# An expert's row transposes traced in front of the next routing round instead of behind it

## The chip, the cores and the metric

The kernel runs on one core of a Trainium2 chip. The metric is the device time of one execution in microseconds (us). Engines: PE is TensorE (matmuls; PEld its weight loads), DVE is VectorE, ACT is ScalarE, POOL is GpSimd, SP is SyncE, which here only issues DMAs.

## The reference

A linear attention with decay gives 3072 tokens of 384 values each; a mixture of 8 experts then works on them. Tokens go to experts by one global greedy order over all (token, expert) scores, with room for 384 tokens per expert:

```python
for t in range(S):                                   # S = 768, per batch and head
    state = alpha[:, :, t, :, None] * state + np.einsum('bhd,bhe->bhde', k[:, :, t], v[:, :, t])
    y[:, :, t] = np.einsum('bhd,bhde->bhe', q[:, :, t], state)
...
logits = x @ w_gate                                  # x: 3072 x 384, 8 experts
order = np.argsort(-logits.flatten())
for idx in order:
    tok, e = (int(idx) // E, int(idx) % E)
    if assigned[tok] >= 0 or counts[e] >= cap:       # cap = 384
        continue
    assigned[tok] = e
    counts[e] += 1
...
for e in range(E):
    mask = assigned == e
    h = np.maximum(x[mask] @ w1[e], 0.0)             # w1[e]: 384 x 1024
    out[mask] = h @ w2[e]                            # w2[e]: 1024 x 384
```

All data is float32.

## The kernel before, in words

**Attention.** The first 150 us or so compute `x` and its scores `L` chunk by chunk; `x` is written to `x_dram` in HBM. The change does not touch this part.

**Routing rounds.** Instead of sorting, the kernel runs 8 rounds. Each round finds the expert that fills up next, and the score at which it does. `search` (line 565) does it digit by digit, in five steps t = 0 to 4: VectorE compares all scores with a table of digit values (`compare`, line 542, tile `cmp`), TensorE counts with 24 small matmuls (line 591), VectorE tests the counts (`g`, line 592), one more matmul sums the test (line 598), VectorE takes the digit (`k`, line 600) and forms the next key (`nd`, line 603). At the end `es`/`ei` (lines 608, 610) hold the expert's number; SP reads it and issues four DMAs for that expert's weights (`weights`, line 518: two halves of `w1r`, line 525, and of `w2r`, line 527; the pool has two buffers for each). `extract` (line 696) turns the round's token set into a list: VectorE builds one-hot tiles (`hot`, line 712), 24 matmuls (line 722) sum them into a PSUM tile `ix`, VectorE makes `idx` of it (line 724), and GpSimd issues three indirect DMAs (line 729) that gather the 384 rows into `xr`, 128 rows each. `update` (line 633) prepares the next round's scores, with the first comparison, `top` and `cmp`, and the tile `o`. The last round, `search_last`, needs no search.

**Experts.** Expert i is the one found by round i. `prep(i)` (line 765) transposes its rows on TensorE in three groups of three (line 779) into a PSUM tile `xt`; ScalarE rounds each group to `xh` (line 782) and VectorE keeps the rest, `xl` (line 784). A float32 product is made of three rounded ones, so weights are split too: `split` (line 746), per block q of 128 hidden values (8 blocks, q = 0 to 7), ScalarE `whi` (lines 751, 752) and GpSimd `wlo` (line 757); seven buffers of each. The `wlo` splits of an expert wait for given comparisons of round i + 1, by the table `BEHIND`. `ffn1` (line 789) runs 9 matmuls per block (line 795), and ScalarE and VectorE make `hh` and `hl` (lines 799, 800); `ffn2` (line 805), two blocks behind, runs 9 matmuls (line 815). The results go to HBM by indirect DMA (line 826).

**What sets the order.** Each engine runs one queue in order. A scheduler fills these queues from the order in which the code is traced and from priorities; inside `tc.high_priority()` a routing round goes ahead of experts' work. Buffers are handed out in the order of tracing: the pool `psx` has one buffer (`bufs=1`, line 147), which serves the attention's transposes, every round's `ix` (line 717, also named `xt`) and every expert's three `xt` (line 770) in turn. A tile of that pool can be written only when the tile traced before it has been read.

The code traces round 0, round 1, then expert 0's `prep` and blocks; then round i + 1 in front of `prep(i)` for each further expert (lines 833 to 850). Between round 0 and expert 0, `spin_after` (line 553) puts some matmuls without use (line 561) on TensorE.

Of the kernel before, what the change touches and what calls it, by code (L numbers as in the profile page):

```python
# [12 lines left out]
ROUTE_AHEAD = 3  # L13
# [14 lines left out]
def gla_moe_kernel(ctx, tc, q, k, v, alpha, w_gate, w1, w2, out):  # L28
# [10 lines left out]
    E = w_gate.shape[1]  # L39
# [469 lines left out]
    def row(x, w=NU):  # L509
        return x[:, :, None].to_broadcast([128, NU, w])  # L510

    def col(x, n=NU):
        return x[:, None, :].to_broadcast([128, n, x.shape[-1]])
# [35 lines left out]
    st = dict(chu=chu0, o=o0, dig=[dig0[:, t] for t in range(nb)])  # L549
# [83 lines left out]
    def update(i):  # L633
        es, v = st["es"], st["v"]
        nt = st["nt"] + 1
        oh = rw.tile([128, 1], F32, name="oh")
        nc.vector.tensor_scalar(oh[:nt], pcs[:nt], st["k"][:nt], None, op0=OP.is_equal)
        gone = st["rt"][:, 40:48]
        with tc.issue_after(st["tri"].ins):
            nc.tensor.matmul(gone, oh[:nt].to_broadcast([nt, 128]), st["cs"][:nt], start=True, stop=True)  # L640
        nc.vector.tensor_reduce(m_c, L, axis=X, op=OP.max)
        nc.vector.scalar_tensor_tensor(sel_c, v, float(CAP), qe_c, op0=OP.is_le, op1=OP.mult)
        val = rw.tile([128, NU, E], BF, name="val")
        if i + 2 < E:
            sg = rw.tile([128, NU], I32, name="sg")
            nc.vector.tensor_scalar(sg, m_c.bitcast(I32), 31, -2 ** 31, op0=OP.arith_shift_right,
                                    op1=OP.bitwise_or)
            nc.vector.scalar_tensor_tensor(asg, sel_c, es, asg, op0=OP.mult, op1=OP.add)
            nc.vector.tensor_tensor(key_c, m_c.bitcast(I32), sg, op=OP.bitwise_xor)  # L649
            nc.vector.tensor_tensor(val, L, row(m_c, E), op=OP.is_equal)  # L650
            nc.vector.tensor_tensor(di_c, key_c[:, None, :].to_broadcast([128, nb, NU]), shifts,
                                    op=OP.logical_shift_right)
            nc.vector.tensor_tensor(di_c, di_c, masks, op=OP.bitwise_and)
            top = rw.tile([128, NU], BF, name="top")
            nc.vector.tensor_scalar(top, di_c[:, 0], 1.0, None, op0=OP.add)
            for _ in compare(i + 1, top, 0):
                pass
            nc.vector.scalar_tensor_tensor(dig_c, di_c[:, 1:], 1.0, scale[:, 1:], op0=OP.add, op1=OP.mult)
            st["dig"] = [top] + [dig_c[:, t] for t in range(nb - 1)]
        else:  # L660
            nc.vector.scalar_tensor_tensor(asg, sel_c, es, asg, op0=OP.mult, op1=OP.add)
            nc.vector.tensor_tensor(val, L, row(m_c, E), op=OP.is_equal)
        nc.vector.tensor_mul(val, val, col(ramp_c))
        nc.vector.tensor_scalar(un_c, asg, 0.0, None, op0=OP.is_equal)
        ch = rw.tile([128, NU], F32, name="ch")
        nc.vector.tensor_reduce(ch, val, axis=X, op=OP.max)
        nc.vector.tensor_sub(rem, rem, gone)
        chu = rw.tile([128, NU], F32, name="chu")
        nc.vector.tensor_mul(chu, ch, un_c)
        nc.vector.scalar_tensor_tensor(rem, cl_c, 8192.0, rem, op0=OP.mult, op1=OP.add)  # L670
        o = rw.tile([128, NU, E], BF, name="o")
        nc.vector.tensor_tensor(o, col(ramp_c), row(chu, E), op=OP.is_equal)
        st.update(chu=chu, o=o, ch=ch)

    def search_last(i):
        es = rw.tile([128, 1], F32, name="es")
        ei = rw.tile([128, 1], I32, name="ei")
        nc.vector.tensor_copy(es, st["ch"][:, 0:1])
        nc.vector.tensor_scalar(ei, es, -1.0, float(E), op0=OP.mult, op1=OP.add)
        weights(i, ei)  # L680
        nc.vector.tensor_add(asg, asg, st["chu"])
        nc.vector.tensor_scalar(ms_c, asg, es, None, op0=OP.is_equal)
        rts = rw.tile([128, 2], BF, name="rts")
        with nc.allow_low_precision(reason="counts of at most 24 ones"):
            nc.vector.tensor_reduce(rts[:, 0:1], ms_c, axis=X, op=OP.add)
        cum = rw.tile([128, 2, NU], F32, name="cum")
        nc.vector.tensor_tensor_scan(cum[:, 0], ones_c, ms_c, 0.0, op0=OP.mult, op1=OP.add)
        rt = fps.tile([128, 64], F32, name="rt")
        nc.tensor.matmul(rt[:, 16:17], tri, rts[:, 0:1], start=True, stop=True)
        offs = rw.tile([128, 2], F32, name="offs")  # L690
        nc.vector.tensor_copy(offs[:, 0:1], rt[:, 16:17])
        v = rw.tile([128, NU], F32, name="v")
        nc.vector.scalar_tensor_tensor(v, cum[:, 0], offs[:, 0:1], ms_c, op0=OP.add, op1=OP.mult)
        st.update(v=v, v1=None)
# [51 lines left out]
    def split(i, q):  # L746
        hi = fp.tile([128, 2, DB, 128], F32R, name="whi", bufs=7)
        lo = fp.tile([128, 2, DB, 128], F32R, name="wlo", bufs=7)
        a = W1R[i][:, :, q * 128:(q + 1) * 128]
        c = W2R[i][:, q].rearrange("p (a b) -> p a b", b=128)  # L750
        nc.scalar.activation(hi[:, 0], a, AF.Copy)  # L751
        nc.scalar.activation(hi[:, 1], c, AF.Copy)
        with ExitStack() as es:
            if i == 0:
                es.enter_context(tc.issue_after(first_gather[0].ins))
            for h, x in enumerate((a, c)):
                y = nc.gpsimd.tensor_sub(lo[:, h], x, hi[:, h])  # L757
                if i + 1 in compared:
                    after = compared[i + 1][BEHIND[2 * q + h]]
                    tc.add_manual_dep(y.ins, after.ins.name,  # L760
                                      mybir.DependencyInfo(mybir.DependencyClass.Sync, mybir.DependencyReason.DATA),
                                      reason="weights split while the search reads one table at a time")
        CH[i, q] = hi, lo

    def prep(i):
        hi = wp.tile([128, DB, CAP], F32R, name="xh")
        lo = fp.tile([128, DB, CAP], F32R, name="xl")
        for b in range(NB):
            bs = slice(b * 128, (b + 1) * 128)
            o = psx.tile([128, DB, 128], F32, name="xt")  # L770
            with ExitStack() as es:
                if i:
                    es.enter_context(tc.issue_after(F2[i - 1, FB - 3].ins))
                else:
                    st["spin"] = spin_after(WARM_IN_ROUTE[1 + b], *st["spin"])
                    for x in st["spin"]:
                        es.enter_context(tc.issue_after(x.ins))
                for d in range(DB):
                    x = nc.tensor.transpose(o[:, d], XR[i][:, b, d * 128:(d + 1) * 128], ident)  # L779
                if i == 0:  # L780
                    st["spin"] = [x]
            nc.scalar.activation(hi[:, :, bs], o, AF.Copy)  # L782
            with tc.high_priority():
                nc.vector.tensor_sub(lo[:, :, bs], o, hi[:, :, bs])
        XH[i], XL[i] = hi, lo
# [45 lines left out]
        scattered.append(st_)  # L831

    route_priority = [0]
    for n in range(E * FB + 2):
        i, q = divmod(n, FB)
        if i < E:
            if q == 0:
                for r in ((0, 1) if i == 0 else (i + 1,) if i + 1 < E else ()):
                    with tc.high_priority():
                        if r < ROUTE_AHEAD:  # L840
                            tc.cur_priority = route_priority[0]
                        with tc.issue_after(st.pop("hot").ins) if "hot" in st else ExitStack():
                            if r:
                                update(r - 1)
                        search(r) if r < E - 1 else search_last(r)
                        extract(r, 1 if r else 2)
                        route_priority[0] = tc.cur_priority
                prep(i)
            split(i, q)
            ffn1(i, q)  # L850
        if n >= 2:
            i, q = divmod(n - 2, FB)
            if i < E - 1 or q < FB - LAST_BLOCKS:
                ffn2(i, [q])
            elif q == FB - 1:
                ffn2(i, list(range(FB - LAST_BLOCKS, FB)))
            while pending:
                scatter()
# [39 lines left out]
```

## Time and profile before

| | |
|---|---|
| median of 3 runs | 474.49 us (472.36 to 476.5) |
| profiled execution | 476.95 us |
| its span, first to last instruction | 475.2 us |
| mean granted TensorE clock | 0.925 |
| busy: PE, PEld, DVE, ACT, POOL | 411.6, 355.9, 293.3, 193.2, 283.3 us |

In the rows of the profile, a line number names the line of the kernel; `out<-in` are tile names; a time in brackets is how long the engine stood idle before the row, and who ended the wait. Timelines give start and length in us from the start of the span. A table of windows gives, for stretches of time, each engine's busy time, then the granted clock (1.00 is full speed), the share of the DMA engines and GB/s. A list of DMA landings gives the time from issue to landing (minimum, median, maximum) of the DMAs it covers. Matmuls overlap one another, so their lengths exceed their pitch.

### The profile page before, as it was taken

To read this page: it belongs to the slowest core of one execution; us is meant where nothing else is said; L and a number is where in the kernel's file an instruction comes from. 1 tells how busy PE (TensorE), PEld (TensorE's weight loads), DVE (VectorE), ACT (ScalarE), POOL (GpSimd) and SP (SyncE) were. 2 spreads that over 40 slices of the span, in tenths; PEclk is the share of its full clock that TensorE was granted. 3 is DMA by queue.
4 is the path that set the end of the run, shared out by engine and by line. 5 is a ranking of instruction groups with operands and counts; after the bars stand their busy time and mean duration, and the time that the engine had idled before them with its cause. 6 is when DMAs were issued, how large, how long until landed. Compare 5 with 4: busy or idle time off the path is not lost.

```text
span 475.2 us, 10764 instructions
## 1 busy us (share of the span) xinstructions
PE 411.6 (87%) x4142; PEld 355.9 (75%) x4142; DVE 293.3 (62%) x836; ACT 193.2 (41%) x453; POOL 283.3 (60%) x292
## 2 busy tenths in 40 slices
PE   6998899887898643489999999999999969999994
PEld 3776677666677522368987988988988959999993
DVE  7987776767735576766865775875875862222210
ACT  2555554544465322013442352352443434554511
POOL 3886656465510056513894697696796796676802
PEclk8799999899999955569988999999999989999998
DMA  8766656566304653620820631721720825410101
GB/s 258 229 205 200 199 174 208 164 202 188 114 2 173 225 185 134 228 89 1 278 73 17 215 102 51 244 82 44 265 69 34 282 84 153 164 51 0 51 0 52
DMA packets 44595, 65.20 MB, mean 137 GB/s; under 512 B 3328, under 2 KB 26880, under 8 KB 44544
## 3 DMA queue, kind: packets, MB, share of 16 engines
q1 hardware_dynamic: 38304, 50.35, 32.5%
q0 software_dynamic: 3072, 9.44, 6.1%
q10 hardware_dynamic: 3168, 4.72, 2.8%
q8 instruction: 33, 0.54, 0.5%
q14 instruction: 18, 0.15, 0.1%
HBM read 55.06 MB, written 9.44 MB: 136 GB/s over the span
## 4 chain that ended last, share of the span: by engine, by line
PE 57%; DVE 20%; DMA 10%; issue 6%; ACT 3%; POOL 1%; POOLq 0%; DVEq 0%; ACTq 0%; SPq 0%
PE h L795 20%; PE y L815 18%; DMA al<-in_alpha_dram 10%; PE rt L591 6%; DVE sc L234 4%; DVE cmp L542 4%; DVE ga L237 3%; PE xt L360 2%; PE y L323 2%; PE xt L779 2%; PE y L317 2%; PE s L268 1%; PE xt L722 1%; ACT xh L782 1%; DVE vi L699 1%
## 5 line engine op out<-in xcount | busy, mean ns | idle before, releaser
L757 POOL TENSOR_TENSOR wlo<-w1r,whi 128x384 fp32r<-128x384 f32 x64 | 67.9, 1061 | 64.1 <-ACT whi L751 58.5
L757 POOL TENSOR_TENSOR wlo<-w2r,whi 128x384 fp32r<-128x384 f32 x64 | 72.2, 1129 | 4.7 <-DVE cmp L542 3.7
L800 DVE SCALAR_TENSOR_TENSOR hl<-h,hh 128x384 fp32r<-128x384 f32 x64 | 35.1, 553 | 57.7 <-ACT hh L799 56.9
L799 ACT ACTIVATE hh<-h 128x384 fp32r<-128x384 f32 x64 | 31.5, 493 | 88.2 <-PE h L795 88.2
L815 PE MATMUL y<-wlo,hh 128*128 128x384 f32 x192 | 67.0, 349 | 0.0
L751 ACT ACTIVATE whi<-w1r 128x384 fp32r<-128x384 f32 x64 | 33.2, 525 | 81.3 <-PE y L815 63.0
L815 PE MATMUL y<-whi,hh 128*128 128x384 f32 x192 | 65.9, 343 | 0.0
L815 PE MATMUL y<-whi,hl 128*128 128x384 f32 x192 | 64.5, 338 | 0.0
L729 POOL DMA_INDIRECT xr<-x_dram,idx x24 | 32.3, 1347 | 42.5 <-DVE scr L649 32.0
L795 PE MATMUL h<-xh,whi 128*128 128x384 f32 x192 | 48.1, 360 | 1.1 <-ACT xh L782 1.0
L795 PE MATMUL h<-xl,whi 128*128 128x384 f32 x192 | 48.6, 354 | 0.0
L795 PE MATMUL h<-xh,wlo 128*128 128x384 f32 x192 | 46.5, 346 | 0.0
L280 POOL TENSOR_SCALAR_AFFINE_SELECT sm<-sm 128x512 f32<-128x512 f32 x36 | 22.4, 637 | 39.5 <-ACT sm L279 38.2
L591 PEld LDWEIGHTS <-cmp 128*128 128x128 bf16 x816 | 30.6, 118 | 19.6 <-DVE cmp L542 14.0
L591 PE MATMUL rt<-o,cmp 128*128 128x8 bf16 x816 | 32.7, 175 | 12.4 <-DVE cmp L542 9.6
L234 DVE TENSOR_TENSOR_SCAN sc<-al,aux 128x516 f32<-128x516 f32 (+1 forms) x26 | 29.7, 1144 | 21.9 <-DMA al<-in_alpha_dram 20.3
L826 POOL DMA_INDIRECT out_dram<-yt,idx x24 | 30.1, 1254 | 20.5 <-ACT yt L819 14.8
L301 ACT ACTIVATE sb<-st,sc 128x48 f32<-128x48 f32 x80 | 25.9, 332 | 33.9 <-DVE st L308 22.2
L542 DVE TENSOR_TENSOR cmp<-nd,iota 128x1536 bf16<-128x1536 bf16 (+4 forms) x32 | 37.0, 1167 | 1.0
L795 PEld LDWEIGHTS h<-xh,whi 128*128 128x128 f32 x192 | 35.4, 199 | 2.9 <-ACT xh L782 2.4
L815 PEld LDWEIGHTS y<-whi,hh 128*128 128x128 f32 x192 | 36.2, 189 | 0.1
L815 PEld LDWEIGHTS y<-wlo,hh 128*128 128x128 f32 x192 | 36.2, 188 | 0.1
(175 smaller groups left out, 838.5 us busy)
## 6 DMA issues: line engine op xcount, KB each, us to landing
w1r<-in_moe_w_dram SPq DMA_DIRECT2D x16, 768.0 KB, 5.6
w2r<-in_moe_w_dram SPq DMA_DIRECT2D x16, 768.0 KB, 8.2
al<-in_alpha_dram SPq DMA_DIRECT2D x24, 256.0 KB, 3.4
raw_k<-in_k_dram SPq DMA_DIRECT2D x24, 256.0 KB, 3.9
raw_q<-in_q_dram SPq DMA_DIRECT2D x24, 256.0 KB, 4.1
vt<-in_v_dram SPq DMA_DIRECT2D x24, 256.0 KB, 2.7
x_dram<-xg ACTq DMA_DIRECT2D x6, 768.0 KB, 3.5
xr<-x_dram,idx POOLq DMA_INDIRECT x24, 3.5
```

Source lines behind the costliest of these rows:

```text
L234: nc.vector.tensor_tensor_scan(sc[:, lo + 1:hi + 1][:, ::-1], a[:, lo + 1:hi + 1][:, ::-1], aux[:, top - 129 * n:top][:, ::-1], 1.0, op0=O ...
L301: nc.scalar.activation(SB[s, u][:, :D], St[p], AF.Copy, scale=ac)
L542: x = nc.vector.tensor_tensor(words(dst, nt, js), keyed(d, nt, js), each(iotas[t], nt, js), op=OP.is_ge)
L591: nc.tensor.matmul(cnt, cmp[:, j // U, :, j % U], o[:, j], start=(j == 0), stop=(j == NU - 1))
L729: last_gather[0] = nc.gpsimd.indirect_dma_start(out=XR[i][:, b], out_offset=None, in_=x_dram, in_offset=bass.IndirectOffsetOnAxis(ap=IDX[i ...
L751: nc.scalar.activation(hi[:, 0], a, AF.Copy)
L757: y = nc.gpsimd.tensor_sub(lo[:, h], x, hi[:, h])
L795: nc.tensor.matmul(o, a[:, 0, d], x[:, d], start=(n == 0), stop=(n == 3 * DB - 1))
L799: nc.scalar.activation(hh, o, AF.Relu)
L800: nc.vector.scalar_tensor_tensor(hl, o, 0.0, hh, op0=OP.max, op1=OP.subtract)
L815: F2[i, q] = nc.tensor.matmul(Y[b], a[:, bs], w[:, 1].rearrange("p a b -> p (a b)"), start=(q == 0 and n == 0), stop=(q == FB - 1 and n == 2))
L826: st_ = nc.gpsimd.indirect_dma_start(out=out, out_offset=bass.IndirectOffsetOnAxis(ap=IDX[i][:, b:b + 1], axis=0), in_=yt, in_offset=None)
```

## The change

The loop body that runs a round becomes a function `route(r)`; the loop calls it at other places. For expert 0 it was: round 0, round 1, `prep(0)`. Now it is: round 0, `prep(0)`, round 1. For further experts it was: round i + 1, `prep(i)`. Now: `prep(i)`, round i + 1. Nothing else is edited.

```diff
     route_priority = [0]
+
+    def route(r):
+        with tc.high_priority():
+            if r < ROUTE_AHEAD:
+                tc.cur_priority = route_priority[0]
+            with tc.issue_after(st.pop("hot").ins) if "hot" in st else ExitStack():
+                if r:
+                    update(r - 1)
+            search(r) if r < E - 1 else search_last(r)
+            extract(r, 1 if r else 2)
+            route_priority[0] = tc.cur_priority
+
     for n in range(E * FB + 2):
         i, q = divmod(n, FB)
         if i < E:
             if q == 0:
-                for r in ((0, 1) if i == 0 else (i + 1,) if i + 1 < E else ()):
-                    with tc.high_priority():
-                        if r < ROUTE_AHEAD:
-                            tc.cur_priority = route_priority[0]
-                        with tc.issue_after(st.pop("hot").ins) if "hot" in st else ExitStack():
-                            if r:
-                                update(r - 1)
-                        search(r) if r < E - 1 else search_last(r)
-                        extract(r, 1 if r else 2)
-                        route_priority[0] = tc.cur_priority
+                if i == 0:
+                    route(0)
                 prep(i)
+                if i + 1 < E:
+                    route(i + 1)
             split(i, q)
             ffn1(i, q)
```

The single `psx` buffer was handed out as ix 0, ix 1, expert 0's three `xt`, ix 2, expert 1's three `xt`, and so on; now as ix 0, expert 0's three, ix 1, expert 1's three, ix 2.

**TensorE after round 0's list is made.** `warm` rows are the matmuls without use, L591 the counts of round 1, `xr_2604` the rows of expert 0. Before, first the place behind round 0's L640, then the place behind round 1's list:

```order
L640 MATMUL rt_2487<-cs_2515,oh_2610 128x8
...
L561 LDWEIGHTS warm_60
L561 MATMUL h_2888<-warm_60 128x384
L591 LDWEIGHTS cmp0_98
...
L722 MATMUL xt_2854<-rhs_2851,hot_2850 128x3
L779 MATMUL xt_2887<-ident_63,xr_2604 128x128 x3
...
L779 MATMUL xt_2907<-ident_63,xr_2604 128x128 x3
L795 MATMUL h_2922<-xh_2885,whi_2916 128x384 x3
```

and now:

```order
L640 MATMUL rt_2487<-cs_2515,oh_2641 128x8
...
L779 MATMUL xt_2612<-ident_63,xr_2604 128x128 x3
...
L779 MATMUL xt_2623<-ident_63,xr_2604 128x128 x3
...
L779 MATMUL xt_2632<-ident_63,xr_2604 128x128 x3
L591 LDWEIGHTS cmp0_98
```

The transposes of expert 0 stood behind the whole of round 1 (its L722 is the end of its list); now they stand ahead of its first count, and the L795 of expert 0 follow that count.

**VectorE at the same place.** The piece of the difference at the start of round 1; `xl` are expert 0's:

```order
 L542 TENSOR_TENSOR cmp_98<-top,iota 128x3072
+L784 TENSOR_TENSOR xl<-xt,xh 128x3x128
 L658 SCALAR_TENSOR_TENSOR scr<-scr,scale 128x96
 L663 TENSOR_TENSOR val<-val,scr 128x192
 L664 TENSOR_SCALAR scr<-asg 128x24
 L666 TENSOR_REDUCE ch<-val 128x24
+L784 TENSOR_TENSOR xl<-xt,xh 128x3x128
```

Two of the three `xl` now stand between steps of the round, the third just before its first L592.

**TensorE from one expert to the next.** The end of a round's list (the last L722), what follows it, and the transposes of the next expert. Before, where `xt_4455` is the list of round 4 and `xr_3943` holds the rows of expert 3:

```order
L722 MATMUL xt_4455<-rhs_4452,hot_4451 128x3
L795 MATMUL h_4188<-xl_3948,whi_4182 128x384 x2
L795 MATMUL h_4188<-xh_3947,wlo_4183 128x384 x3
...
L779 MATMUL xt_4488<-ident_63,xr_3943 128x128 x3
...
L779 MATMUL xt_4500<-ident_63,xr_3943 128x128 x3
L591 LDWEIGHTS cmp0_98
```

Now, where `xt_5014` is the list of round 5 and `xr_5041` holds the rows of expert 5, gathered by that same list:

```order
L722 MATMUL xt_5014<-rhs_5011,hot_5010 128x3
L795 MATMUL h_5237<-xl_4751,whi_5231 128x384 x2
L795 MATMUL h_5237<-xh_4750,wlo_5232 128x384 x3
...
L779 MATMUL xt_5291<-ident_63,xr_5041 128x128 x3
...
L779 MATMUL xt_5297<-ident_63,xr_5041 128x128 x3
L815 MATMUL y2_5134<-whi_5231,hl_5248 128x384
L591 LDWEIGHTS cmp0_98
```

The transposes used rows gathered one round earlier, 14 matmuls (L795, L815) behind the list; now they use the rows of the list just made, 32 matmuls behind it. The second group stands 8 matmuls behind the first, and the first count of the next round (L591) follows that second group, no longer the third.

**ScalarE in the middle of an expert.** `hh_4679` and `hh_4708` are blocks 5 and 6 of expert 3; `whi_5045`, `whi_5074` and `whi_5112` are splits for blocks 0, 1 and 2 of expert 4. Before:

```order
L799 ACTIVATE hh_4679<-h_4669 128x384
L751 ACTIVATE whi_5112<-w1r_4419 128x384
L752 ACTIVATE whi_5112<-w2r_4420 128x384
L799 ACTIVATE hh_4708<-h_4698 128x384
L751 ACTIVATE whi_5144<-w1r_4419 128x384
```

and now:

```order
L799 ACTIVATE hh_4679<-h_4669 128x384
L751 ACTIVATE whi_5045<-w1r_4439 128x384
L751 ACTIVATE whi_5074<-w1r_4439 128x384
L751 ACTIVATE whi_5112<-w1r_4439 128x384
L752 ACTIVATE whi_5045<-w2r_4440 128x384
L752 ACTIVATE whi_5074<-w2r_4440 128x384
L752 ACTIVATE whi_5112<-w2r_4440 128x384
L799 ACTIVATE hh_4708<-h_4698 128x384
```

The splits were spread, a pair behind each `hh`; now three of `w1r` and then three of `w2r` stand between the `hh` of block 5 and that of block 6. SP's queue, which issues the weights' DMAs, has the same rows in the same order.

## Prediction

> **What bounds the kernel now.** I read first the table of windows, cut at the moments when TensorE opens a routing round or an expert; the cuts come from the chain of waits. Columns: stretch, its length, busy time of PE, PEld, DVE, ACT and POOL (instructions in brackets), granted clock, DMA share, GB/s.
>
> ```profile
> 175.94:205.35 29.41, 11.33 (x166) 8.46 (x166) 20.47 (x63) 4.18 (x9) 18.20 (x18) 0.50 0.56 190
> 205.35:241.31 35.96, 35.02 (x307) 32.01 (x308) 25.27 (x77) 13.17 (x29) 16.99 (x15) 0.95 0.32 104
> 241.31:280.08 38.77, 36.74 (x310) 33.87 (x309) 26.12 (x74) 13.80 (x31) 26.81 (x23) 0.91 0.33 113
> 280.08:314.66 34.58, 33.53 (x309) 30.83 (x309) 24.77 (x74) 13.73 (x31) 26.80 (x23) 1.00 0.37 127
> 314.66:349.24 34.58, 33.57 (x309) 30.85 (x309) 24.73 (x74) 13.73 (x31) 26.75 (x23) 1.00 0.37 126
> 349.24:387.19 37.95, 33.71 (x309) 30.72 (x307) 28.45 (x81) 13.08 (x30) 29.66 (x27) 0.99 0.36 123
> 387.19:416.19 29.00, 28.94 (x178) 27.56 (x178) 7.08 (x15) 13.35 (x30) 20.41 (x21) 0.95 0.45 145
> 416.19:442.85 26.66, 26.60 (x154) 25.66 (x154) 6.13 (x12) 13.73 (x31) 18.91 (x20) 1.00 0.06 23
> 442.85:475.20 32.35, 25.31 (x144) 24.88 (x144) 5.00 (x9) 7.89 (x17) 10.70 (x11) 0.95 0.10 38
> ```
>
> From 205 us on TensorE is nearly full: 33.53 of 34.58 us in a stretch that holds one expert and one round, 26.60 of 26.66 where an expert runs alone. The hole is the first row: round 1 by itself, 29.41 us with TensorE busy 11.33 and a clock of 0.50. What opens and closes it stands in TensorE's timeline (start, length, work, then the idle time before it and its releaser):
>
> ```profile
> 175.94 0.96 PE L591 MATMUL rt<-o,cmp 128*128 128x8 bf16 x24 [2.49 <-DVE o L672]
> 199.12 0.90 PE L779 MATMUL xt<-ident,xr 128*128 128x128 f32 x3 [0.25 <-DVE idx L724]
> 203.87 0.90 PE L779 MATMUL xt<-ident,xr 128*128 128x128 f32 x3 [1.13 <-DVE xl L784]
> 205.35 1.97 PE L795 MATMUL h<-xh,whi 128*128 128x384 f32 x5 [0.58 <-ACT xh L782]
> ```
>
> Expert 0's first transposes start right after `idx` of round **1**, though they need only the rows gathered by round 0. The rows had been there long before (GpSimd's gathers, and the landing time that the list of DMA issues gives for the last of the three):
>
> ```profile
> 171.16 1.17 POOL L729 DMA_INDIRECT xr<-x_dram,idx  x1 [31.99 <-DVE scr L649]
> 172.63 2.44 POOL L729 DMA_INDIRECT xr<-x_dram,idx  x1 [0.30 <-issue]
> 175.38 0.95 POOL L729 DMA_INDIRECT xr<-x_dram,idx  x1 [0.30 <-DVE ch L666]
> DMA to landing us min/median/max: 4.6/4.6/4.6
> ```
>
> The last block lands at 175.38 + 4.6 = 180.0. So expert 0 sits 19 us on data that is there, held by the one `psx` buffer: its `xt` tiles are traced behind round 1's `ix`.
>
> **Part 1, the head.** No instruction is added or removed, and SP's queue keeps its order, so each DMA is issued as often and in the same turn; what moves is the turn of expert 0's transposes and all that follows from it. The change lets round 0's `ix`, then expert 0's three `xt`, then round 1's `ix` use that buffer in turn. The order of TensorE confirms it: three groups of transposes, then the first L591 of round 1. Third group: from 180.0, 0.90 us at the low clock as in the row at 203.87, so L591 of round 1 (0.96 us) starts at 180.9 instead of 175.94, and the first L795 at about 182, instead of 205.35: 23.4 us earlier. Round 1 itself loses 5 us, because VectorE's `xl` now stands between its steps and waits for the transposes; only the expert counts here, since TensorE is the full engine from then on. Splits are no obstacle: GpSimd's first `wlo` ended at 177.3 in these conditions, and the splits of the other blocks are tied to the tables of round 1 as before:
>
> ```profile
> 176.34 1.01 POOL L757 TENSOR_TENSOR wlo<-w1r,whi 128x384 fp32r<-128x384 f32 x1
> ```
>
> Bounds: no better than the landing at 180.0, which puts the first L795 near 181 (24 us earlier); at worst each of the two earlier groups is late by one more slot wait of 1.13 us, near 184 (21 us). I take 23.4, because every time in it is a row.
>
> The stretch that follows is like the one at 205.35: 35.96 us, of which 0.94 idle. New at its end is that expert 1's rows come from round 1, which has just ended. TensorE has 18 matmuls between L722 and the transposes (18 x 0.174 us, 1.56 / 9 by the L815 row of the next part: 3.1 us); the gather needs about 4.2 (next part). About 1 us of wait, much the size of the idle time that it replaces. So round 2 opens at 182 + 36 = 218, where round 3 opened at 241.3 before: **-23.3 us**.
>
> **Part 2, one more loaded expert.** Before, rounds 2 to 6 ran beside experts 0 to 4, and expert 6 ran free. Now rounds 1 to 6 run beside experts 0 to 5. One stretch of 26.66 becomes one of 34.58: **+7.9 us**. The stretches of 37.95 (with the end of round 6 and round 7) and 29.00 are kept, each with the same work.
>
> **Part 3, the boundary.** This is what the old order hid. The gather for expert i+1 was issued a whole expert ahead; now it runs between L722 and the transposes of the same boundary. Rows of one boundary: timelines of VectorE, GpSimd and TensorE, two rows of the chain of waits (L815 and the last), and the landing times of all 24 gathers (minimum, median, maximum):
>
> ```profile
> 306.88 0.16 DVE L724 TENSOR_SCALAR idx<-xt 128x3 int32<-128x3 f32 x1 [0.45 <-PE xt L722]
> 308.55 0.98 POOL L729 DMA_INDIRECT xr<-x_dram,idx  x1 [0.16 <-issue]
> 309.83 2.47 POOL L729 DMA_INDIRECT xr<-x_dram,idx  x1 [0.30 <-issue]
> 312.61 0.95 POOL L729 DMA_INDIRECT xr<-x_dram,idx  x1 [0.30 <-issue]
> DMA to landing us min/median/max: 3.1/3.5/5.8
> 307.81 1.56 PE y L815 x9
> 309.22 0.49 PE L779 MATMUL xt<-ident,xr 128*128 128x128 f32 x3
> 314.11 0.55 PE L779 MATMUL xt<-ident,xr 128*128 128x128 f32 x3 [0.93 <-DVE xl L784]
> 314.66 0.86 PE rt L591 x24
> ```
>
> Count from the end of L722, 306.8. `idx` at +0.2; the gathers were behind GpSimd's splits until +1.7, and by the order they can go when `idx` is there. Issued at about +0.5, +1.8 and +3.1, landing 3.5 us later: +4.0, +5.3, and +6.6 (+8.1 where one takes 2.47 us). TensorE's new order has 32 matmuls in front of the first group, 8 more to the second: 32 x 0.174 = +5.6, then +7.5; the third is about +10. All three land in time, with 0.5 to 2 us to spare. VectorE's `o` was ready at +7.8; L591 of the next round stands behind the second group, which ends near +8.0, and one matmul, at +8.3 instead of +7.9 (314.66). So about +0.5 us for each of the five boundaries that remain: **+2.5 us**. Lower end: the 0.93 us that the third group waited is saved, -0.5 each. Upper end: the longest landing, 5.8, on a gather behind one of 2.47 us: 5.8 + 3.1 + 1.5 = +10.4, and L591, or the expert's first L795, 2 us late. I take the value near the lower end, since the medians leave room.
>
> Of the weights every DMA is issued at the same point of the round, but now one expert later in use. SP's issue of the first halves, with the landing of each:
>
> ```profile
> 299.44 0.38 SPq L525 DMA_DIRECT2D w1r<-in_moe_w_dram  x1
> DMA to landing us min/median/max: 4.7/4.7/4.7
> 300.08 0.37 SPq L527 DMA_DIRECT2D w2r<-in_moe_w_dram  x1
> DMA to landing us min/median/max: 6.1/6.1/6.1
> 303.82 0.49 ACT L799 ACTIVATE hh<-h 128x384 fp32r<-128x384 f32 x1 [0.56 <-PE h L795]
> ```
>
> They land at 304.1 and 306.2. ScalarE's new order has three splits of each half in front of block 6's `hh`; three splits of `w2r` cost about 1.3 us, so `hh` can start at 307.5, where it stood at 303.82. The expert now runs some 2 to 3 us later against its round, which takes most of that; and TensorE has 27 matmuls (4.7 us) queued before it needs this `hh`. I cost it at nothing; the cover is that queue, and without it the price is 3.7 us at each boundary, the upper end here.
>
> **Sum.** -23.3 + 7.9 + 2.5 = -12.9 us. The profiled execution took 476.95 us (span 475.2), which gives 464.1; it lies 2.5 us above the median of the runs, 474.49. From the median: **461.6 us**.
>
> **The clock.** One term I leave unchanged. The stretch at 241.31 is 4.2 us longer than its neighbours, at clock 0.91. The windows that cost it:
>
> ```profile
> 239.60:243.00 3.40, 2.47 (x34) 1.97 (x32) 1.74 (x7) 2.28 (x6) 3.38 (x4) 1.00 0.43 116
> 243.00:246.70 3.70, 3.70 (x15) 3.65 (x14) 2.89 (x4) 0.49 (x1) 3.49 (x3) 0.54 0.03 7
> 250.10:253.50 3.40, 2.29 (x33) 1.72 (x31) 2.59 (x3) 0.49 (x1) 1.14 (x2) 1.00 0.05 19
> 253.50:257.00 3.50, 3.50 (x13) 3.18 (x13) 1.37 (x3) 1.08 (x3) 2.71 (x2) 0.51 0.00 0
> 313.40:316.80 3.40, 2.69 (x35) 2.44 (x36) 1.84 (x8) 1.76 (x5) 3.39 (x5) 1.00 0.31 95
> ```
>
> TensorE busy 2.47 or 2.29 of 3.40 us is followed by half a clock for 3.5 us; busy 2.69 is not (the stretch from 314.66 has clock 1.00). Each costs 2.1 us. A boundary thus lies close to the edge: I assume two such drops again. [...]
>
> **The rivals.**
> The clock never drops at a boundary: for it, the new order fills the place where the third group waited 0.93 us with matmuls; against it, two drops in the old trace. Then the 4.2 us go too and the boundaries cost nothing: -23.3 + 7.9 - 4.2 = -19.6, 455 us.
> Every boundary drops the clock: for it, gather waits and L591 now lie close together and 2.47 us busy sufficed; against it, 313.40. Six drops instead of two add 4 x 2.1 = 8.4: about 470 us, within 1% of no change.
> Slower, by ScalarE's queue: at each of the six boundaries `hh` of block 6 stands behind `w2r`, TensorE starves, and the pause brings a clock drop. Price per boundary 3.7 + 2.1 us; six make 34.8 less the 4.2 already paid, so -15.4 + 30.6 = +15, 490 us. It decides from 15.4 / 6 = 2.6 us per boundary on. For it: `hh` can start only 3.7 us later than it did. Against it: 4.7 us of queued matmuls and the shift of the expert.
> That the change does nothing is excluded by the order of TensorE.
>
> **How the numbers follow.** Forecast 0.55, no drops 0.20, all drops 0.14, slower 0.11. A measurement of this kernel tells about 1% from no change. Faster by over 1% (under 469.7): forecast, no drops, and a small part of the third, 0.78. Within 1%: 0.12. Slower by over 1%: 0.10. The range 453 to 471 holds the first three cases with the bounds of Part 1 (2 us) and Part 3, and leaves out the slower one and some of the tails.
>
> **What would show it.** In the new trace: first L795 at 181 to 184; the granted clock back at 1.0 some 4 us after it; rounds' first L591 35 us apart beside experts 1 to 4; idle time before L779 under 1.5 us and released by DVE or a gather; two stretches without a round instead of three. Wrong would be: `hh` L799 waiting for a w2r transfer, or L779 waiting over 2 us for `xr` at each boundary, or a clock of 0.5 after each of them.

## The result and the profile after

The changed kernel takes 471.74 us in the median of 20 runs (469.43 to 475.67), the kernel before 475.94 us beside it (20 runs, 472.36 to 481.83). The ratio is 0.9927, with a 95% interval of 0.9899 to 0.9955: about 3.5 us faster, where 12.9 were forecast. 471.74 lies just above the range. Some executions fall into a second, slower state; the ratios here and below leave these out, so they are not the quotients of the medians.

The profiled execution of the changed kernel took 475.40 us, 3.7 above its median; its span is 473.6 us, that of before 475.2. The table of windows of the changed kernel, cut where TensorE opens a round (its first L591) or, in the first row and the last three, an expert (its first L795); columns as in the prediction's table:

```profile
183.07:222.80 39.73, 37.13 (x287) 34.21 (x285) 23.92 (x74) 15.03 (x34) 20.96 (x20) 0.88 0.37 129
222.80:259.78 36.98, 34.44 (x309) 31.84 (x308) 23.64 (x74) 12.45 (x29) 21.73 (x21) 0.95 0.35 118
259.78:294.50 34.72, 33.64 (x301) 30.84 (x299) 24.53 (x74) 12.00 (x27) 23.44 (x23) 0.95 0.38 126
294.50:328.99 34.49, 33.77 (x311) 30.92 (x311) 24.95 (x74) 13.90 (x31) 24.22 (x23) 1.00 0.36 127
328.99:363.40 34.41, 33.73 (x310) 30.90 (x308) 24.91 (x74) 13.89 (x31) 24.09 (x23) 1.00 0.36 127
363.40:410.25 46.85, 37.29 (x320) 33.52 (x319) 34.33 (x84) 17.71 (x39) 34.39 (x35) 0.90 0.49 168
410.25:440.95 30.70, 30.65 (x177) 29.52 (x177) 6.29 (x13) 12.18 (x27) 18.29 (x20) 0.87 0.09 28
440.95:473.60 32.65, 25.30 (x144) 24.87 (x144) 5.00 (x9) 7.89 (x17) 10.76 (x11) 0.93 0.10 37
```

The big hole at the head is gone: first L795 at 183.07 instead of 205.35. The odd row is the sixth, 46.85 us, with the end of round 6 and round 7. It stands where before had 37.95. TensorE is busy 37.29 us of it, so it loses 9.6 us there, and the clock is 0.90 in it and 0.87 in the row behind.

What TensorE waits for there is in its timeline (start, length, work, idle time before it and its releaser), at the second of expert 6's three groups of transposes (the expectation of the first experiment calls it the third):

```profile
406.29 0.90 PE L779 MATMUL xt<-ident,xr 128*128 128x128 f32 x3 [7.86 <-DVE xl L784]
```

`xl` was not late by its own work. VectorE's timeline of the changed kernel shows one long instruction in front of it, `vi` of round 7, with `hot` behind that, and GpSimd's timeline shows what ran at that time:

```profile
395.01 8.30 DVE L699 TENSOR_SCALAR vi<-v 128x24 int32<-128x24 f32 x1
404.02 1.75 DVE L712 TENSOR_TENSOR hot<-wb,iota 128x3072 f16<-128x3072 bf16 x1
405.68 0.55 DVE L784 TENSOR_TENSOR xl<-xt,xh 128x384 fp32r<-128x384 f32 x1
```
```profile
394.60 2.96 POOL L757 TENSOR_TENSOR wlo<-w2r,whi 128x384 fp32r<-128x384 f32 x3
397.51 1.02 POOL L757 TENSOR_TENSOR wlo<-w1r,whi 128x384 fp32r<-128x384 f32 x1
...
402.28 0.98 POOL L757 TENSOR_TENSOR wlo<-w2r,whi 128x384 fp32r<-128x384 f32 x1
403.43 1.00 POOL L826 DMA_INDIRECT out_dram<-yt,idx  x1 [0.17 <-issue]
```

24 numbers per partition take 8.30 us, and they end when a run of nine splits ends on GpSimd: 403.31 against 402.28 + 0.98 = 403.26. The same instruction in the trace of before, VectorE's row first, then GpSimd's, then TensorE's (there the third group waits):

```profile
381.02 4.08 DVE L699 TENSOR_SCALAR vi<-v 128x24 int32<-128x24 f32 x1
```
```profile
381.21 1.03 POOL L757 TENSOR_TENSOR wlo<-w1r,whi 128x384 fp32r<-128x384 f32 x1
...
384.08 0.98 POOL L757 TENSOR_TENSOR wlo<-w2r,whi 128x384 fp32r<-128x384 f32 x1
385.23 1.00 POOL L826 DMA_INDIRECT out_dram<-yt,idx  x1 [0.17 <-issue]
```
```profile
386.06 0.55 PE L779 MATMUL xt<-ident,xr 128*128 128x128 f32 x3 [3.73 <-DVE xl L784]
```

So the stall is old: four splits and 4.08 us before, nine splits and 8.30 us now. The table holds the forecast's times (from its own terms: 218 for round 2, one stretch of 38.77 and three of 34.58 with 0.5 at each of four boundaries up to round 6, then 37.95 + 0.5, 29.00 and 32.35), the changed kernel's, and those of the run with nine splits held back, which comes below. All are us from the span's start.

| TensorE opens | forecast | changed kernel | splits held |
|---|---|---|---|
| first L795 | 182 | 183.07 | 179.84 |
| round 2 | 218 | 222.80 | 217.41 |
| round 6 | 362.5 | 363.40 | 355.36 |
| expert 6 | 400.9 | 410.25 | 393.62 |
| expert 7 | 429.9 | 440.95 | 421.21 |
| end | 462.3 | 473.60 | 453.90 |

Up to round 6 the changed kernel is 0.9 us off the forecast, but by two errors that cancel: it is 4.8 us late at round 2, and the four stretches behind it take 3.9 us less than forecast. 10.4 of the 11.3 us that are missing at the end are lost between round 6 and the end.

### The profile page after: what moved, and what is told of

Read it like the earlier page. It is cut to its first block, busy times and chain, and to the rows that moved or that the text cites. A ratio compares the mean times of both kernels' runs of the same rounds, so it can differ in the third digit from the quotient of the medians.

```text
span 473.6 us, 10767 instructions
## 1 busy us (share of the span) xinstructions
PE 415.7 (88%) x4142; PEld 359.4 (76%) x4142; DVE 294.0 (62%) x836; ACT 192.8 (41%) x453; POOL 269.2 (57%) x292
## 4 chain that ended last, share of the span: by engine, by line
PE 58%; DVE 18%; DMA 12%; issue 7%; ACT 3%; POOL 1%; SPq 0%; POOLq 0%; DVEq 0%; ACTq 0%
PE h L795 20%; PE y L815 17%; DMA al<-in_alpha_dram 9%; PE rt L591 6%; DVE sc L234 4%; DVE ga L237 3%; DVE cmp L542 2%; PE y L317 2%; PE xt L779 2%; PE y L323 2%; DMA xr<-x_dram,idx 2%; DVE vi L699 2%; PE s L268 1%; PE xt L722 1%; PE xt L360 1%
## 5 line engine op out<-in xcount | busy, mean ns | idle before, releaser
L757 POOL TENSOR_TENSOR wlo<-w2r,whi 128x384 fp32r<-128x384 f32 x64 | 64.7, 1013 | 31.6 <-DVE cmp L542 30.1
L757 POOL TENSOR_TENSOR wlo<-w1r,whi 128x384 fp32r<-128x384 f32 x64 | 64.5, 1010 | 15.1 <-ACT whi L751 14.9
L815 PE MATMUL y<-wlo,hh 128*128 128x384 f32 x192 | 67.2, 350 | 0.0
L815 PE MATMUL y<-whi,hh 128*128 128x384 f32 x192 | 67.1, 349 | 0.0
L815 PE MATMUL y<-whi,hl 128*128 128x384 f32 x192 | 66.1, 344 | 0.0
L751 ACT ACTIVATE whi<-w1r 128x384 fp32r<-128x384 f32 x64 | 32.2, 521 | 55.1 <-PE y L815 38.1
L795 PE MATMUL h<-xl,whi 128*128 128x384 f32 x192 | 50.2, 364 | 0.0
L795 PE MATMUL h<-xh,wlo 128*128 128x384 f32 x192 | 50.0, 361 | 0.0
L795 PE MATMUL h<-xh,whi 128*128 128x384 f32 x192 | 48.4, 360 | 1.8 <-ACT xh L782 1.7
L826 POOL DMA_INDIRECT out_dram<-yt,idx x24 | 27.4, 1142 | 31.0 <-ACT yt L819 26.5
L795 PEld LDWEIGHTS h<-xh,whi 128*128 128x128 f32 x192 | 35.6, 201 | 5.2 <-ACT xh L782 3.3
L795 PEld LDWEIGHTS h<-xh,wlo 128*128 128x128 f32 x192 | 36.9, 203 | 0.0
L815 PEld LDWEIGHTS y<-wlo,hh 128*128 128x128 f32 x192 | 36.9, 192 | 0.1
L795 PEld LDWEIGHTS h<-xl,whi 128*128 128x128 f32 x192 | 36.8, 204 | 0.2
L815 PEld LDWEIGHTS y<-whi,hh 128*128 128x128 f32 x192 | 36.9, 192 | 0.1
```

The source lines that it names most:

```text
L795: nc.tensor.matmul(o, a[:, 0, d], x[:, d], start=(n == 0), stop=(n == 3 * DB - 1))
L815: F2[i, q] = nc.tensor.matmul(Y[b], a[:, bs], w[:, 1].rearrange("p a b -> p (a b)"), start=(q == 0 and n == 0), stop=(q == FB - 1 and n == 2))
L826: st_ = nc.gpsimd.indirect_dma_start(out=out, out_offset=bass.IndirectOffsetOnAxis(ap=IDX[i][:, b:b + 1], axis=0), in_=yt, in_offset=None)
```

## The experiments

Theory (the expectations call it the port theory; what `vi` waits for inside the chip, no row shows): `vi` in its last form (SBUF to SBUF, one input) doesn't get done while GpSimd's splits follow each other, 8.30 us beside nine and 4.08 beside four. In rounds 0 to 6 the other form runs, with one input in PSUM, in 0.18 us each time. Rival A: the last round's form is new to VectorE, and its code comes late. Rival B: the weights in flight (DMA share 0.99 while `vi` lasts) slow VectorE.

**Another source for vi.** Round 7's `v` goes to a PSUM slot, in the changed kernel:

```
-        v = rw.tile([128, NU], F32, name="v")
+        v = v1_c
```

> The changed kernel; round 7's v is written to a PSUM slot instead of an SBUF tile, nothing else is changed by hand. Port theory (vi, reading and writing SBUF alone, cannot start while GpSimd's splits follow one another, and lasts until their run ends: 395.01 to 403.31 against splits from 394.60 to 403.26): vi takes about 0.2 us, TensorE's 7.86 us in front of expert 6's third transposes go, the half clock from 400.95 to 418.01 shrinks to one drop of 3.4 us or none, and expert 6's first L795 stands about 35 us behind the opening of round 6 instead of 46.85. 11.7 us, and 2 to 4 us of clock behind it: about 457 us, 454 to 461. Rival A (the first use of this instruction waits for its code): the form with a PSUM source is as new as the old one, vi stays above 3 us, 468 to 474. Rival B (the weights in flight at that time slow VectorE): the transfers are the same, vi stays above 3 us, 468 to 474.

Measured: 466.72 us, ratio 0.9784 (0.9729 to 0.9838). Timelines of VectorE and GpSimd in this run:

```profile
389.39 0.17 DVE L699 TENSOR_SCALAR vi<-scr 128x24 int32<-128x24 f32 x1
390.28 9.03 DVE L712 TENSOR_TENSOR hot<-wb,iota 128x3072 f16<-128x3072 bf16 x1
```
```profile
389.01 2.95 POOL L757 TENSOR_TENSOR wlo<-w2r,whi 128x384 fp32r<-128x384 f32 x3
...
396.70 0.98 POOL L757 TENSOR_TENSOR wlo<-w2r,whi 128x384 fp32r<-128x384 f32 x1
397.85 2.33 POOL L826 DMA_INDIRECT out_dram<-yt,idx  x1 [0.17 <-issue]
```

`vi` is as short as the theory says, beside the same splits, and both rivals are wrong about it. But 466.7 us is 10 us more than the expected 457: the stall moved on to the next instruction that takes its inputs from SBUF. `hot`, with two of them, takes 9.03 us instead of 1.75. The run of splits is over at 396.70 + 0.98 = 397.68, and `hot` ends 1.63 us behind that, at 399.31, about its own length later.

**The same line in the kernel before.**

> The kernel before with the same line: round 7's v in PSUM. Port theory: vi falls from 4.08 to about 0.2 us, the 3.73 us wait in front of the third transposes at 386.06 goes, and with it perhaps the half clock from 386.66 to 390.07 (1.7 us): 475.9 less 3.5 to 5.5, about 471.5 us, 470 to 473. The change is then worth about 14 us between two kernels that both lack the stall, near the 12.9 that was forecast. Rivals A and B: no difference, 475 to 477, vi at 4 us.

Measured: 474.97 us, ratio 0.9974 (0.9944 to 1.0003). Expected were 471.5; the reason is the same, in the same two instructions:

```profile
382.29 0.18 DVE L699 TENSOR_SCALAR vi<-scr 128x24 int32<-128x24 f32 x1
383.70 4.34 DVE L712 TENSOR_TENSOR hot<-wb,iota 128x3072 f16<-128x3072 bf16 x1
```

These two runs say what suffers, and that it isn't one instruction. They don't yet price the stall.

**The splits held back.** The kernel already ties splits to the tables of the next round (`compared`, `BEHIND`); round 7 compares nothing, so expert 6's splits have nothing to wait for. Here `vi` of round 7 fills that place, for all of expert 6's splits but the first three of `w1r`:

```
-            nc.vector.tensor_scalar(vi, st["v"], -1.0, None, op0=OP.add)
+            compared[i] = [nc.vector.tensor_scalar(vi, st["v"], -1.0, None, op0=OP.add)] * 5
...
-                if i + 1 in compared:
+                if i + 1 in compared and (i < 6 or h or q > 2):
```

> The changed kernel with vi as it is (SBUF to SBUF); nine of expert 6's splits on GpSimd (those behind the gathers) are made to wait until vi is done. Every engine keeps its order of instructions. Port theory: GpSimd is idle when vi starts, vi takes about 0.2 us, the nine splits run from about 395.3 to 404, and the time is that of the kernel with v in PSUM within 2 us: 455 to 462. Rivals A and B: vi takes its 8 us without any split beside it, the splits end 8 us later than before, 472 to 481.

Measured: 457.13 us, ratio 0.9598 (0.9535 to 0.9660). VectorE, then GpSimd, then two windows of that time (columns as above) in this run:

```profile
387.07 0.17 DVE L699 TENSOR_SCALAR vi<-v 128x24 int32<-128x24 f32 x1
387.96 2.04 DVE L712 TENSOR_TENSOR hot<-wb,iota 128x3072 f16<-128x3072 bf16 x1
```
```profile
387.38 4.47 POOL L757 TENSOR_TENSOR wlo<-w2r,whi 128x384 fp32r<-128x384 f32 x3 [0.66 <-issue]
```
```profile
387.07:393.62 6.55, 5.22 (x32) 4.25 (x30) 4.01 (x11) 5.09 (x12) 6.24 (x5) 1.00 1.01 353
393.62:405.30 11.68, 11.68 (x86) 11.42 (x87) 2.93 (x6) 3.85 (x8) 10.42 (x12) 1.00 0.40 142
```

The form of `vi` is the old one, used here for the first time too, and 353 GB/s of transfers are in flight with a DMA share of 1.01; it takes 0.17 us. That ends rivals A and B. With one more condition on those splits and no instruction moved on any engine, the kernel is 13 to 16 us faster than the changed one, by the ratios of this run and of a second one below.

**Fewer splits held**, a run between the two: the same with the condition `(i < 6 or q > 2)`, so three splits of `w2r` go ahead of `vi`.

> As the run with nine splits held, but only the last six wait for vi; three w2r splits follow the gathers as before, from 394.6 to 397.6. Port theory: vi ends with these three, 2.4 to 2.6 us after its start at about 395.0, a length between 0.2 (nine held) and 8.30 (none held); TensorE waits about 2 us for the third transposes, and the time is 2 to 4 us above the run with nine held. Rivals A and B: vi takes 8 us, as without any hold.

Measured, in a single execution: 463.13 us. VectorE, GpSimd and TensorE:

```profile
388.83 2.56 DVE L699 TENSOR_SCALAR vi<-v 128x24 int32<-128x24 f32 x1
```
```profile
388.38 2.96 POOL L757 TENSOR_TENSOR wlo<-w2r,whi 128x384 fp32r<-128x384 f32 x3
391.53 1.02 POOL L757 TENSOR_TENSOR wlo<-w1r,whi 128x384 fp32r<-128x384 f32 x1 [0.19 <-DVE vi L699]
```
```profile
394.68 0.55 PE L779 MATMUL xt<-ident,xr 128*128 128x128 f32 x3 [2.43 <-DVE xl L784]
```

`vi` ends at 391.39, the three splits at 391.34. So its length follows the run's: 0.17 us with none, 2.56 with three, 4.08 with four, 8.30 with nine (and 0.76 with one, in the last run below: `vi` from 386.68 to 387.44, a split from 386.40 to 387.42). The time is 6 us above the run with all held, where 2 to 4 were expected: behind the 2.43 us wait the clock stayed at half for 10 us (in TensorE's timeline three L779 take 0.90 us at 396.40, three L795 1.16 us up to the group at 404.81, and 0.68 us at 406.41).

**The kernel before without the stall.** The four splits behind the gathers (expert 5's blocks 4 and 5) wait for `vi`; in short form:

```
+        for y in SPLITS[5][8:12]:
+            tc.add_manual_dep(y.ins, vi_op.ins.name, ...)
```

`SPLITS` is a list that `split` fills, two entries for each block; `vi_op` is the instruction of L699.

> The kernel before, vi as it is; the four splits of expert 5 that follow the last but one gathers on GpSimd (blocks 4 and 5, at 381.21 to 385.06 in the old trace) wait until vi is done. No engine's order changes. Port theory: vi takes 0.2 instead of 4.08 us, hot about 2 us, the 3.73 us wait in front of the third transposes goes, with or without its half clock (1.7 us): 4 to 6 us less than the kernel before, ratio 0.987 to 0.992. Against this kernel, the changed one with its splits held (457 us) is then worth 14 to 15 us, near the 12.9 of the forecast: the forecast's terms were right and the stall took the gain. Rival (the change itself is worth only 4 us, and holding splits helps any kernel by 15): this run falls by 15 too, to about 461.

Measured: 471.57 us, ratio 0.9945 (0.9911 to 0.9980). Its windows of round 6 to expert 6:

```profile
349.18:383.28 34.10, 33.61 (x308) 30.73 (x306) 24.58 (x81) 13.15 (x30) 26.18 (x24) 1.00 0.39 132
383.28:411.22 27.94, 27.88 (x177) 26.40 (x177) 7.07 (x15) 13.35 (x30) 24.27 (x25) 1.00 0.47 156
```

37.95 became 34.10 and 29.00 became 27.94, 4.9 us less in these two profiles. By the ratio, which rests on more executions, the stall cost the kernel before 2.6 us (1 to 4), less than the 4 to 6 expected; the rival, 461, is out.

**The changed kernel with the splits held, beside it.**

> The changed kernel with expert 6's splits held behind vi, a second time, beside the kernel before with its splits held: 455 to 461 us, ratio 0.955 to 0.967 to the kernel before, and 13 to 16 us under the kernel before with its splits held, if the port theory holds; equal to it by the rival.

Measured: 457.62 us, ratio 0.9656 (0.9607 to 0.9705). Against the run before it on the same chip the change is worth 471.57 - 457.62 = 13.95 us when neither kernel has the stall.

**Held until hot is done.** The entry in `compared` is `hot`'s last instruction instead of `vi`.

> As the run with expert 6's splits held behind vi, but held until hot is done as well. [...] Port theory: hot 1.75 us, no split longer than 1.05 us around it; the end moves by 0 to 0.5 us, 455 to 461, the same as with the hold behind vi within the measurement. A time 3 us or more above that would say that the held splits come too late for TensorE.

Measured: 455.97 us, ratio 0.9614 (0.9566 to 0.9661), the same within the measurement, and with it the best version here, faster than both kernels. `hot` takes 1.75 us, but GpSimd's stores of expert 5 now stand in another place of its order. Its windows at the head and in the stretch of the stall:

```profile
179.96:217.16 37.20, 34.52 (x288) 31.66 (x286) 23.93 (x74) 14.93 (x34) 21.01 (x20) 0.95 0.40 138
217.16:251.12 33.96, 32.91 (x306) 30.46 (x303) 23.57 (x73) 12.30 (x29) 21.50 (x21) 1.00 0.38 128
...
354.97:393.05 38.08, 36.00 (x320) 32.76 (x319) 26.24 (x84) 17.59 (x39) 26.85 (x27) 1.00 0.50 169
```

**The later moves alone**, with the splits held:

```
                 if i == 0:
                     route(0)
+                    route(1)
                 prep(i)
-                if i + 1 < E:
+                if 1 < i + 1 < E:
                     route(i + 1)
```

> One part of the change alone, with expert 6's splits held behind vi: rounds 0 and 1 both in front of expert 0's transposes as before, but from expert 1 on each expert's transposes stand in front of the next round. The head keeps its hole (first L795 at about 205), expert 0 runs without a round (26.7 us), five stretches with a round follow (34.5 each, the last 38 with round 7), then 27.6 and 32.7 from the run with the splits held: 205.4 + 26.7 + 138 + 38.3 + 27.6 + 32.7 = 468.7 us of span, 470 us, ratio 0.98 to 0.99 to the kernel before. So the gain of the whole change would lie in the head, and the later moves cost nothing. If the later moves cost 0.5 us or more at each boundary, or bring a clock drop at each, this run is 473 to 480.

Measured: 477.43 us, ratio 1.0044 (0.9991 to 1.0097): no gain, and 7 us above what was expected. TensorE's timeline and two windows:

```profile
208.23 0.99 PE L591 MATMUL rt<-o,cmp 128*128 128x8 bf16 x24
240.29 1.15 PE L795 MATMUL h<-xh,whi 128*128 128x384 f32 x5 [0.72 <-ACT xh L782]
241.29 0.93 PE L722 MATMUL xt<-rhs,hot 128*128 128x3 f16 x23
```
```profile
240.29:276.49 36.20, 35.24 (x306) 32.16 (x306) 25.31 (x75) 13.62 (x31) 25.85 (x23) 0.95 0.36 121
276.49:312.18 35.69, 33.65 (x306) 30.73 (x307) 26.31 (x75) 13.63 (x31) 25.57 (x23) 1.00 0.36 123
```

My picture of this run was wrong. Round 2 opens at 208.23, beside expert 0 as before (208.08), because rounds 0 to 2 take the priority of the head (`ROUTE_AHEAD`) wherever they are traced; no expert runs alone at first, and a round stays one expert further ahead. What does change is the turn in the `psx` buffer: a round's L722 now comes behind the next expert's transposes, and the stretches are 35.7 and 36.2 us (the latter at a clock of 0.95) instead of 34.58. So this run doesn't price the boundaries of the change. It does show that the later moves, in this form, bring nothing without the first one. That the gain is the head's is argued from the first L795, which stands 22 us earlier in the changed kernel; no run has the first move alone.

## Why the prediction was wrong, point by point

**The failed step** is the sentence of Part 2 "The stretches of 37.95 (with the end of round 6 and round 7) and 29.00 are kept, each with the same work." Their own work is nearly the same (in the first, 320 matmul records against 309, since a round's first count now stands earlier in its expert); its neighbours are not. Before, rounds 6 and 7 ran beside expert 4, and GpSimd had four splits of expert 5 left behind round 6's gathers, the table `BEHIND` having spread the others over that round. Now they run beside expert 5, and the splits are those of expert 6, whose weights have just landed and which no comparison holds back; nine stand behind the gathers. The stretches measured 46.85 and 30.70, +8.4 (against 37.95 + 0.5) and +1.7; with the splits held they are 38.26 and 27.59. By the ratios the changed kernel loses 13 to 16 us to the stall (0.9927 against 0.9656 and 0.9598), the kernel before 2.6. So the change is worth 13.95 us where neither kernel has the stall and about 3.5 where both have it; the difference, about 10 us, is what the forecast lacked (471.74 - 461.6 = 10.1).

That 38.26 lies near the 38.45 of the forecast is in part luck: the old stretch of 37.95 held 3.85 us of stall (34.10 without it), which the forecast took over unseen.

Two rows that the prediction quotes showed that something was wrong in that stretch: VectorE was busy 28.45 us in the 37.95, and 24.73 in the one ahead, for seven instructions more. The table said where to look, and `vi` with 4.08 us was there. I took an old stretch as a constant without asking what was in it, and no rival spoke of VectorE against GpSimd.

What the runs show of the wait: among nine splits in a row `vi` takes 0.17 us with its source in PSUM and 8.30 from SBUF; `hot`, with both inputs in SBUF, takes 9.03 us in the first experiment and 4.34 in the second, instead of 1.75. By what means GpSimd's splits hold VectorE up is not shown. One split takes about 1 us (0.98 to 1.03 in the rows above), but `vi` waited for the whole run: for it, the number of splits that follow each other, not the length of one, is what a forecast had to count.

**Part 1, the head, was right; the stretch behind it was put too short.** First L795 at 183.07 (182 forecast, 181 to 184 allowed). The profiled execution reached round 0's L722 2.15 us later than that of before (170.71 against 168.56), so from there on the head took 1.1 us less than forecast; in the three runs with all nine splits held the first L795 came at 179.84, 180.11 and 179.96. Round 2 opened at 222.80 in the changed kernel, but at 217.41, 217.32 and 217.16 in those, where 218 was forecast. That the latter come so near is in part luck: their stretch takes 37.2 to 37.6 us instead of 36, from a start 2 us earlier. The 222.80 has the later start and a drop of the clock behind the wait for expert 1's rows:

```profile
216.57 0.84 PE L779 MATMUL xt<-ident,xr 128*128 128x128 f32 x3 [2.17 <-DMA xr<-x_dram,idx]
```
```profile
216.60:220.10 3.50, 3.50 (x13) 3.50 (x14) 1.70 (x6) 0.93 (x3) 2.83 (x3) 0.51 0.20 56
```

I had said about 1 us of wait there. The row of the gather in the chain of waits (start, length) gives the reason, 4.83 us to the landing and not 3.5:

```profile
211.61 4.83 DMA xr<-x_dram,idx
```

**Part 2's +7.9 was right:** six stretches hold a round from 183.07 on, and two have none.

**Part 3, +0.5 at a boundary, was too much.** The stretches 34.72, 34.49 and 34.41 are those of before (34.58); the true term lies between the value taken and the lower end, near 0. The groups of TensorE's instructions of the changed kernel from 183 us on (count, then busy time and mean ns, then idle time before them by releaser) show how little the rows cost:

```profile
L815 PE MATMUL y<-whi,hh 128*128 128x384 f32 x192 | 67.1, 349 | 0.0
...
L779 PE MATMUL xt<-ident,xr 128*128 128x128 f32 x63 | 12.2, 304 | 11.4 <-DVE xl L784 8.3 <-DMA xr<-x_dram,idx 3.1
```

All transposes together waited 3.1 us for gathered rows, 2.17 of it at expert 1; 7.86 of the 8.3 behind `xl` are the stall.

**The clock** was the other size that was off: two drops were assumed up to round 6; the changed kernel's execution had three there (granted clock 0.51 from 216.60 to 220.10 us, 0.51 from 226.80 to 230.20, 0.50 from 264.40 to 267.80). In the stretches that open with expert 0 and with round 2 its clock was 0.88 and 0.95, that of the run held until `hot` is done 0.95 and 1.00; the mean over the span was 0.934, and 0.958 to 0.971 in the four runs with expert 6's splits held, in whole or in part. Without the stall 456 to 458 us were measured. All cases of the prediction contain the old stall, so these are to be held against the forecast less the 2.6 to 4.9 us that it cost the kernel before, 457 to 459, and not against the 455 of "the clock never drops at a boundary", which becomes 450 to 452. That the result lies near the 470 of "every boundary drops the clock" is chance: three boundaries out of six were clean (granted clock 1.00 from 268 to 400 us).

**The slower rival**, ScalarE's queue, didn't come: the L815 row just shown has no idle time before the matmuls that need `hh`, and the last stretches ahead of round 6 run at the old 34.5 us.

## What to carry to other kernels

Before a stretch of the old trace is taken over into a sum, look for the instruction in it that is far longer than its like, and find out what ends it; if that is another engine's queue, ask what that queue holds after the move. In these profiles such a wait stands as busy time of the instruction that waits (`vi`, 8.30 us), so the views of idle time and releasers name its engine and not the one that holds it up. A move that brings two engines' work together in time can have a price even where neither gets more work, here about 10 us. Where a kernel ties one engine's work to another's by hand, check that the table of ties still covers the steps that the move makes neighbours.

## What the runs showed of the hardware that was not expected

`vi` did not wait for one split but for the whole run of them: it started within 0.5 us of the first of nine and got in behind the last; in the kernel before its row starts 0.19 us ahead of the first of four, and it ended with the last all the same. `hot` went both ways. In the run with nine splits held it came at 387.96, during the first split (from 387.38), took 2.04 us, and three splits took 4.47 instead of 2.96; in the run with `v` in PSUM it came at 390.28, during the second, and waited for the last. The trace of before shows the first case in rounds 2 to 6, each time with four splits in a row: `hot` comes about 0.4 us into the first and takes 2.2 us, and the second split takes 2.5. In round 6:

```profile
372.49 2.23 DVE L712 TENSOR_TENSOR hot<-wb,iota 128x3072 f16<-128x3072 bf16 x1
```
```profile
372.09 1.02 POOL L757 TENSOR_TENSOR wlo<-w1r,whi 128x384 fp32r<-128x384 f32 x1 [1.53 <-ACT whi L751]
373.06 2.54 POOL L757 TENSOR_TENSOR wlo<-w2r,whi 128x384 fp32r<-128x384 f32 x1
```

So in these traces `hot` got in behind the first split of a run when it came during that one, and waited for the last when it came during the second; `vi` came during the first too and waited for the last. Why they differ stays open.

The wait alone does not decide the clock. At expert 1's rows TensorE waited 2.17 us in the changed kernel and 2.04 in the run with nine splits held (2.15 in the run with six held and in the one held until `hot` is done). The first was followed by the half clock shown above, the others by none: behind the waits of 2.15 the next three L779 take 0.49 us in both, and in the run with nine splits held the windows are

```profile
210.50:212.60 2.10, 0.11 (x1) 0.00 (x0) 1.38 (x1) 0.52 (x1) 2.10 (x1) 1.00 0.40 111
212.60:216.10 3.50, 3.45 (x22) 3.45 (x23) 1.70 (x6) 2.32 (x6) 3.07 (x4) 1.00 0.20 56
```

And a half clock can outlast the wait by far. Behind the 7.86 us in the changed kernel TensorE was busy again from 406.3 on, and the clock stayed at half for another 11.7 us:

```profile
401.00:406.30 5.30, 0.01 (x1) 0.01 (x1) 5.20 (x8) 0.00 (x0) 3.27 (x4) 0.50 0.74 266
406.30:418.00 11.70, 10.71 (x55) 9.60 (x56) 1.97 (x6) 3.54 (x8) 6.80 (x7) 0.50 0.26 78
```

That is the +1.7 of the stretch behind and part of the +8.4: what the stall costs is its wait and the slow matmuls after it.
